# Whole 128x128 tiles in place of the half tiles of 64 in an attention and expert kernel

## The chip, the cores and the metric

The kernel runs on one core of one Trainium2 chip. The metric is the device time of one execution in microseconds (us). The core's engines each run an instruction queue of their own, in order: TensorE (in the profile PE, its weight loads PEld), VectorE (DVE), ScalarE (ACT), GpSimd (POOL) and SyncE (SP), which issues the transfers.

## The reference

Three stages follow one another on 8 batches of 576 tokens: attention over keys and values that are averaged in groups of 8, four causal attention experts of which each token takes two, and a mixing of tokens and channels.

```python
# attention: 8 heads, 576 queries, 72 pooled keys
k_p = k.reshape(B, H, Sp, pool, D).mean(axis=3)
scores = scale * np.matmul(q, k_p.transpose(0, 1, 3, 2))
attn = softmax(scores)
x = np.matmul(attn, v_p)
# experts: 4 of them, each with one causal head of 64
for e in range(E):
    a = softmax(causal(scale * (x @ wq[e]) @ (x @ wk[e]).T))
    out += gate[e] * (a @ (x @ wv[e]) @ wo[e])
# mixing
theta = x @ w_theta
y = w_tok_r @ (x * cos(theta)) + w_tok_i @ (x * sin(theta))
u = x + y
out = u + max(u @ w_ch, 0)
```

## The kernel before

A planner (class `Plan`) records every instruction with what it reads and writes, and a price for each (`price`). `issue` then takes the instructions in the order in which a model of the engines would run them: the earliest modelled start first, and of several the lowest key. Keys come from two tables, `PARTS` and `SHIFT`, that stand in the file as constants. What comes out is one fixed order for each engine. As all instructions are issued at one place in `issue`, the profile gives line L413 to all of them, and they are told apart by the names of their tiles.

Each batch goes through stage A (the first attention), the projections, and stage B (the experts). The planner weaves stage B of batch b with stage A and the projections of batch b + 1. Stage C (the mixing) comes last, for all batches; the weights of its stage are decoded earlier, in between.

576 is 4 times 128 and 64 more. So each batch ends in a half tile:

- `load_q` loads the queries in five tiles, `qraw`. The fifth has 64 queries.
- `attn_half` takes each tile of queries: 4 float32 products of the queries with the pooled keys (`s<-kbd,qraw`, the queries being the weights that TensorE holds, each product two matmul instructions), the exponentials in `pp`, then the normalised probabilities `pm` (64 keys of each of 8 heads) and `pq` (the other 8 keys). TensorE transposes them, four times 128 columns of `pm` and one time 64 columns of `pq`, into `t`; from there ScalarE and VectorE write the two exact parts of `pa` and of `pr`. `pq` is a tile of 64 columns for every tile of queries, so its transpose uses half of the array's columns in all five. The fifth tile works with 64 rows.
- `proj_v` makes the values `v` and the gates' logits by tile of tokens: 12 matmuls `acc<-wvs,xT` in each tile, with 64 columns in the fifth.
- `turn` transposes the experts' probabilities (`pev`, `pod`) into `pt0`, `pt1`; the last 64 keys of the last 64 queries (i = 8) become `pt2`, a tile of 64 partitions, by a transpose of 64 columns.
- `heads` multiplies them with the values: matmuls `acc<-pt,v`, and for the last 64 keys four matmuls of 64 rows and 64 moving columns in each of the two pairs of experts, by 2 parts and 2 experts.

In the profile's forms, 128\*128 are the rows and columns of the array that an instruction uses; 128\*64 uses half of the columns, 64\*128 half of the rows, and 64\*64 half of both. In stage C the last 64 tokens of two batches are put together, so that no half tile is left there.

Of the kernel before, what the change touches and what calls it, by code (L numbers as in the profile page):

```python
# [20 lines left out]
S = 576  # L21
# [74 lines left out]
class View:  # L96
    """a tile that is made when its first instruction is issued, or a part of it"""
# [50 lines left out]
class Pool:  # L148
    """a tile pool that is opened and closed among the instructions"""
# [44 lines left out]
class Plan:  # L194
    """Records the instructions with what they read and write, and issues them in the order in which a
    model of the engines would run them: the earliest start first, of several the lowest key."""
# [59 lines left out]
        # a bank is taken only when what empties it can go ahead  # L256
# [19 lines left out]
        # the time in which the weights of a product come in, while the one before it runs  # L276
# [55 lines left out]
    # from the end of an instruction to the start of one of another engine (in TensorE, of its weights' load)  # L332
# [10 lines left out]
    def issue(self):  # L343
# [4 lines left out]
        # the tiles of a ring are taken in turn, but for those of PSUM  # L348
# [17 lines left out]
        while len(order) < len(self.ops):  # L366
# [21 lines left out]
            if o.eng == "PE":  # L388
                # the clock is halved after a stretch of little work
# [29 lines left out]
def body(ctx: ExitStack, tc, qT, kT, vm, vr, wqk, wvg, wo, woT, wth, wtok, wch, out):  # L419
# [8 lines left out]
    def mm3(acc, lhs, rhs, first, last):  # L428
        """acc += lhsᵀ rhs, each operand as its two exact parts"""
# [50 lines left out]
    # ---------------------------------------------------------------- loads of one batch  # L480
    ld = {}

    def load(b):
        """the loads of one batch; those of the first take buffers that have no use yet, to wait for nothing"""
# [14 lines left out]
        def load_q():  # L499
            for o in range(0, S, 128):  # L500
                t = awork.tile([128, 4, 128], F32, name="qraw", bufs=3)
                m = min(128, S - o)
                D.dma_start(t[:, :, :m], qT[b][:, :, o:o + m])
# [27 lines left out]
    # ---------------------------------------------------------------- constants  # L531
    # what the scores of 64 queries get: NEG in the last 64 columns where the key comes after the query
# [5 lines left out]
    # hm[8 h' + k, h] = 1 where h' = h, for each half of the partitions  # L538
# [8 lines left out]
    # before[e, j] = 1 where j < e  # L547
# [16 lines left out]
    pt2 = [keep.tile([64, 2, 64], F32R, name=f"pt2{c}") for c in range(2)]  # L564
# [6 lines left out]
    # ---------------------------------------------------------------- weights of the first two stages  # L571
# [26 lines left out]
        # the sign, and 0 where float32 has no such number  # L598
# [15 lines left out]
    # the weights that are decoded early, in slack time, and kept in DRAM till they are wanted  # L614
# [11 lines left out]
    # ---------------------------------------------------------------- stage A  # L626
# [42 lines left out]
    def attn_half(b, h, rb):  # L669
        q0, n = HALF[h]  # L670
        tiles = [(o, min(128, n - o)) for o in range(0, n, 128)]
        pa = [awork.tile([128, 4, 320], F32R, name=f"pa{c}", bufs=1) for c in range(2)]
        pr = awork.tile([128, 320], F32R, name="pr", bufs=1)
        for o, m in tiles:
# [3 lines left out]
            for c in range(2):  # L678
                s_ = ps.tile([128, 512], F32, name="s", bufs=4)[:m, :288]
                for p in (2 * c, 2 * c + 1):  # L680
                    T.matmul(s_[:, (p % 2) * 144:(p % 2) * 144 + 144], ld[b][1][(q0 + o) // 128][:, p, :m],
# [3 lines left out]
                V.tensor_reduce(mx[:m], sv, axis=AX.X, op=OP.max, negate=True)  # L685
                if (q0 + o) // 128 in WHOLE[b > 0]:
                    V.tensor_tensor(pp[:m, 4 * c:4 * c + 4], sv, mx[:m, :, None].to_broadcast([m, 4, 72]), op=OP.add)
                    continue
                V.tensor_scalar(mx[:m], mx[:m], 1.0 / 64, None, op0=OP.mult)
                for g in range(4):  # L690
                    A.activation(pp[:m, 4 * c + g], sv[:, g], AF.Exp, bias=mx[:m, g:g + 1], scale=1.0 / 64,
                                 accum_out=l[:m, 4 * c + g:4 * c + g + 1])
            if (q0 + o) // 128 in WHOLE[b > 0]:
                A.activation(pp[:m], pp[:m], AF.Exp, scale=1.0 / 64)
                V.tensor_reduce(l[:m], pp[:m], axis=AX.X, op=OP.add)
            V.tensor_scalar(l[:m], l[:m], 1e-9, 8.0, op0=OP.add, op1=OP.mult)
            V.reciprocal(l[:m], l[:m])
            pm = awork.tile([128, 8, 64], F32, name="pm")
            pq = awork.tile([128, 8, 8], F32, name="pq")
            X = on(b, f"pm{(q0 + o) // 128}")  # L700
            X.tensor_tensor(pm[:m], pp[:m, :, 0:64], l[:m, :, None].to_broadcast([m, 8, 64]), op=OP.mult)
            X.tensor_tensor(pq[:m], pp[:m, :, 64:72], l[:m, :, None].to_broadcast([m, 8, 8]), op=OP.mult)
            pl.lane = "qt"
            t4 = ps.tile([128, 4, 128], F32, name="t")
            for p in range(4):
                T.transpose(t4[:, p, :m], pm[:m, 2 * p:2 * p + 2].rearrange("q g k -> q (g k)"), ident[:m, :m])
            A.copy(pa[0][:, :, o:o + m], t4[:, :, :m])
            V.tensor_tensor(pa[1][:, :, o:o + m], t4[:, :, :m], f(pa[0][:, :, o:o + m]), op=OP.subtract)
            t1 = ps.tile([128, 4, 128], F32, name="t")
            T.transpose(t1[:64, 0, :m], pq[:m].rearrange("q g k -> q (g k)"), ident[:m, :m])  # L710
            A.copy(pr[0:64, o:o + m], t1[:64, 0, :m])
            V.tensor_tensor(pr[64:128, o:o + m], t1[:64, 0, :m], f(pr[0:64, o:o + m]), op=OP.subtract)
# [11 lines left out]
    # ---------------------------------------------------------------- projections  # L724
# [28 lines left out]
    def proj_v(b, hs=(0, 1)):  # L753
# [4 lines left out]
        for t in [t for h in hs for t in ((0, 1), (2, 3, 4))[h]]:  # L758
            h, o = (0, 128 * t) if t < 2 else (1, 128 * t - 256)
            m = 128 if t < 4 else 64  # L760
            acc = ps.tile([128, 512], F32, name="acc")
            for kt in range(4):
                mm3(acc[:m, :260], [x[:, kt, o:o + m] for x in xT[b, h]], [w[:, kt] for w in wv_s],
                    kt == 0, kt == 3)
            a = [acc[:m, 128 * p:128 * p + 128].rearrange("k (e d) -> k e d", e=2) for p in range(2)]
            for p in range(2):
                A.copy(v[p][:m, t, :, 0], a[p])
            for p in range(2):
                V.tensor_tensor(v[p][:m, t, :, 1], a[p], f(v[p][:m, t, :, 0]), op=OP.subtract)
            V.tensor_copy(lg[:m, t], acc[:m, 256:260])  # L770
# [30 lines left out]
    # ---------------------------------------------------------------- stage B  # L801
    cnt = [0, 0]

    def scores(b, p, i, l):
# [8 lines left out]
        for c0, m in parts:  # L813
# [7 lines left out]
            # a = -(a + mask), and the lowest of it  # L821
# [6 lines left out]
    def norm(b, p, units, l):  # L828
        """divides the exponentials of one or two units by their sums, and weighs them with the gates"""
# [10 lines left out]
    def turn(b, p, i, pb, c0):  # L840
# [12 lines left out]
        if i == 8:  # L853
            t = ps.tile([128, 4, 128], F32, name="t")
            T.transpose(t[:64, 0], pb[:, 512:576], ident)
            src = t[:64, 0].rearrange("k (e q) -> k e q", e=2)
            A.copy(pt2[0], src)
            V.tensor_tensor(pt2[1], src, f(pt2[0]), op=OP.subtract)

    def heads(b, p, h):  # L860
# [5 lines left out]
        for e in range(2):  # L866
# [74 lines left out]
    # ---------------------------------------------------------------- stage C  # L941
# [17 lines left out]
    # wo w_theta, which takes the gated heads straight to theta  # L959
# [18 lines left out]
    def loadc(b):  # L978
# [7 lines left out]
        if b % 2 == 0:  # L986
            # the last 64 queries of two batches
# [11 lines left out]
    def mix(b):  # L999
        """x2, theta and the turned x2 of one batch"""  # L1000
# [156 lines left out]
```

## Time and profile before

| | |
|---|---|
| median of 3 runs | 1006.52 us (1005.34 to 1011.48) |
| span of the profiled execution | 1006.9 us |
| PE busy | 941.3 us (93%) |
| DVE busy | 692.6 us (69%) |
| ACT busy | 577.2 us (57%) |
| POOL busy | 519.4 us (52%) |

The span is that of one execution taken by the profiler. The ends of matmuls are modelled, each some 0.2 to 0.4 us after its start, so PE counts as busy while it only waits for a pipeline; what a matmul costs its queue is the time from its start to the start of the next one, which the timeline shows. The timeline merges instructions of one kind that follow each other: start, length from the first start to the last end, and the count.

### The profile page before, as it was taken

The page shows a single profiled execution, that of the slowest core. Times are in us where ns is not written, and L with a number is a line of the kernel's source. Part 1 is how long each engine was busy: PE and PEld are TensorE (multiplying, and loading weights), DVE is VectorE, ACT ScalarE, POOL GpSimd, SP SyncE. Part 2 cuts the span into 40 slices and gives each one's busy share as a digit, 9 for nine tenths or more (in the row PEclk, how much of TensorE's full clock was granted, in tenths as well). Part 3 has the DMA queues.
Part 4 walks back from the last instruction along what each step waited for, and adds up shares of the span by engine and source line. Part 5 has one row for each costly group of instructions (what it writes and reads, how often), then busy time and mean ns, then how long its engine had stood idle before and what let it go on. Part 6 is the DMA issues. An engine that isn't in the chain of part 4 may idle for free.

```text
span 1006.9 us, 19100 instructions
## 1 busy us (share of the span) xinstructions
PE 941.3 (93%) x6512; PEld 873.5 (87%) x6512; DVE 692.6 (69%) x1939; ACT 577.2 (57%) x1824; POOL 519.4 (52%) x641
## 2 busy tenths in 40 slices
PE   4889899999999999999998998999999999999998
PEld 3778789898888888989976798988999899999998
DVE  8899988989877898787779956174535726264421
ACT  4468777877868688686667634153434534353420
POOL 8877667574865837534254665352444435161420
PEclk9999999999999999999999999999999999999999
DMA  8444244343433422312175412020020202010001
GB/s 264 134 127 134 90 119 125 97 127 99 125 98 92 123 74 58 101 38 83 35 251 189 153 54 84 1 68 27 30 61 13 77 1 69 1 36 13 30 19 48
DMA packets 72033, 84.81 MB, mean 84 GB/s; under 512 B 14080, under 2 KB 54528, under 8 KB 71936
## 3 DMA queue, kind: packets, MB, share of 16 engines
q1 hardware_dynamic: 71936, 83.59, 28.2%
q8 instruction: 52, 0.85, 0.3%
q14 instruction: 45, 0.37, 0.1%
HBM read 57.29 MB, written 26.28 MB: 83 GB/s over the span
## 4 chain that ended last, share of the span: by engine, by line
PE 56%; DVE 28%; ACT 6%; issue 3%; POOL 3%; DMA 3%; SPq 0%; DVEq 0%; POOLq 0%; ACTq 0%
PE acc L413 42%; PE s L413 10%; PE t L413 4%; DVE s L413 3%; DVE zf L413 2%; DVE pt L413 2%; DVE d_raw L413 2%; DVE mx L413 2%; DVE th L413 2%; DVE r L413 2%; ACT th L413 1%; DVE qbd L413 1%; DMA d_raw<-in_wch_dram 1%; DMA vraw<-in_vm_dram 1%; DVE pa L413 1%
## 5 line engine op out<-in xcount | busy, mean ns | idle before, releaser
L413 PE MATMUL acc<-toks,z 128*128 128x288 f32 x1536 | 229.2, 296 | 2.0 <-DVE z L413 1.6
L413 PEld LDWEIGHTS acc<-toks,z 128*128 128x128 f32 x1536 | 215.3, 188 | 7.1 <-DVE z L413 2.0
L413 PE MATMUL acc<-xT,wqs 128*128 128x256 f32 (+1 forms) x768 | 136.4, 307 | 12.8 <-DVE qbd L413 8.9
L413 POOL TENSOR_TENSOR us<-u,us 128x288 fp32r<-128x288 f32 x64 | 54.9, 858 | 142.6 <-ACT us L413 142.6
L413 PEld LDWEIGHTS acc<-xT,wqs 128*128 128x128 f32 x768 | 109.0, 189 | 17.9 <-issue 10.8
L413 POOL TENSOR_TENSOR z<-zf,z 128x512 fp32r<-128x512 f32 x60 | 83.3, 1403 | 76.5 <-ACT z L413 76.5
L413 PE MATMUL acc<-us,chs 128*128 128x288 f32 x768 | 118.7, 301 | 3.7 <-ACT chs L413 1.9
L413 PEld LDWEIGHTS acc<-us,chs 128*128 128x128 f32 x768 | 110.6, 190 | 9.5 <-ACT chs L413 2.5
L413 DVE TENSOR_TENSOR u<-acc,xt 128x288 f32<-128x288 f32 x64 | 29.1, 455 | 119.8 <-PE acc L413 119.7
L413 PE MATMUL s<-kb,qbd 128*128 128x288 f32 (+8 forms) x480 | 110.7, 326 | 0.6 <-ACT kb L413 0.6
L413 POOL TENSOR_SCALAR pev<-pev,lb,G 128x64 f32<-128x64 f32 (+4 forms) x80 | 50.7, 634 | 99.6 <-DVE lb L413 40.4
L413 ACT CAST us<-u 128x288 fp32r<-128x288 f32 x64 | 27.6, 431 | 111.4 <-DVE u L413 111.1
L413 PE MATMUL acc<-pt,v 128*128 128x320 f32 (+3 forms) x448 | 80.6, 299 | 3.7 <-ACT pt L413 1.1
L413 ACT ACTIVATE pp<-s,mx 128x72 f32<-128x72 f32 (+1 forms) x232 | 73.3, 328 | 14.8 <-DVE mx L413 13.3
L413 PEld LDWEIGHTS acc<-pt,v 128*128 128x128 f32 (+1 forms) x448 | 68.5, 189 | 14.4 <-ACT pt L413 2.1
L413 ACT CAST pt<-t 128x512 fp32r<-128x512 f32 (+4 forms) x160 | 66.7, 431 | 23.3 <-PE t L413 21.9
L413 DVE TENSOR_TENSOR pt<-t,pt 128x512 fp32r<-128x512 f32 (+4 forms) x160 | 75.1, 482 | 6.1 <-ACT pt L413 5.5
L413 DVE CUSTOM_DVE_ANT_0 s<-s,mask 128x64 f32<-128x64 f32 (+2 forms) x144 | 65.6, 459 | 17.6 <-PE s L413 16.9
L413 PEld LDWEIGHTS s<-kb,qbd 128*128 128x128 f32 x480 | 74.6, 190 | 2.7 <-ACT kb L413 0.8
L413 PE MATMUL acc<-wvs,xT 128*128 128x260 f32 (+1 forms) x480 | 71.2, 290 | 2.6 <-DVE logit L413 1.9
L413 PE MATMUL s<-kbd,qraw 128*128 128x144 f32 (+1 forms) x320 | 62.4, 306 | 8.2 <-POOL hm L413 6.8
L413 PEld LDWEIGHTS acc<-wvs,xT 128*128 128x128 f32 (+1 forms) x480 | 60.7, 179 | 4.3 <-issue 1.8
(171 smaller groups left out, 2211.3 us busy)
## 6 DMA issues: line engine op xcount, KB each, us to landing
out_dram<-o SPq DMA_DIRECT2D x64, 144.0 KB, 1.8
kraw<-in_kT_dram SPq DMA_DIRECT2D x15, 576.0 KB, 4.2
qraw<-in_qT_dram SPq DMA_DIRECT2D x32, 256.0 KB, 3.3
yraw<-ygD SPq DMA_DIRECT2D x16, 512.0 KB, 4.0
vraw<-in_vm_dram SPq DMA_DIRECT2D x15, 512.0 KB, 4.4
d_raw<-in_wtok_dram SPq DMA_DIRECT2D x18, 288.0 KB, 2.9
toks<-tokD SPq DMA_DIRECT2D x18, 288.0 KB, 5.5
ygD<-yg SPq DMA_DIRECT2D x32, 160.0 KB, 2.6
```

The source lines that it names most:

```text
L413: o.ins = o.fn(*[a.real() if isinstance(a, View) else a for a in o.args], **{k: a.real() if isinstance(a, View) else a for k, a in o.kw.it ...
```

## The change

Every half tile becomes a whole one. The fifth tile of queries, keys and tokens starts 64 earlier, at 448, and covers tokens 448 to 575, of which the first 64 are done a second time and not used again (`n_` picks the new ones; the logits take partitions 64 to 127). `pt2` gets 128 partitions, of which the first 64 are zero, set once at the start. `pq` gets 128 columns, of which the last 64 are zero, set once; it is no longer taken from a ring of two but is one of two fixed tiles, by the parity of the tile of queries. The transposes are then 128 by 128. `PARTS`, `SHIFT` and the planner stay as they were. What of the diff takes comments out is not shown.

```diff
         def load_q():
...
-                m = min(128, S - o)
-                D.dma_start(t[:, :, :m], qT[b][:, :, o:o + m])
+                o = min(o, S - 128)
+                D.dma_start(t, qT[b][:, :, o:o + 128])
...
-    pt2 = [keep.tile([64, 2, 64], F32R, name=f"pt2{c}") for c in range(2)]
+    pt2 = [keep.tile([128, 2, 64], F32R, name=f"pt2{c}") for c in range(2)]
+    for t in pt2:
+        P.memset(f(t[:64]), 0.0)
+    pqs = [keep.tile([128, 2, 8, 8], F32, name=f"pq{c}") for c in range(2)]
+    for t in pqs:
+        P.memset(t[:, 1], 0.0)
...
     def attn_half(b, h, rb):
...
-        for o, m in tiles:
+        for o, new in tiles:
...
-                    T.matmul(s_[:, (p % 2) * 144:(p % 2) * 144 + 144], ld[b][1][(q0 + o) // 128][:, p, :m],
+                    T.matmul(s_[:, (p % 2) * 144:(p % 2) * 144 + 144], ld[b][1][(q0 + o) // 128][:, p],
                              kbd[:, p].rearrange("d e k -> d (e k)"), start=True, stop=True)
...
-            pq = awork.tile([128, 8, 8], F32, name="pq")
+            pq = pqs[(q0 + o) // 128 % 2]
...
-            X.tensor_tensor(pq[:m], pp[:m, :, 64:72], l[:m, :, None].to_broadcast([m, 8, 8]), op=OP.mult)
+            X.tensor_tensor(pq[:, 0], pp[:, :, 64:72], l[:, :, None].to_broadcast([128, 8, 8]), op=OP.mult)
             pl.lane = "qt"
+            n_ = slice(128 - new, 128)
             t4 = ps.tile([128, 4, 128], F32, name="t")
             for p in range(4):
-                T.transpose(t4[:, p, :m], pm[:m, 2 * p:2 * p + 2].rearrange("q g k -> q (g k)"), ident[:m, :m])
+                T.transpose(t4[:, p], pm[:, 2 * p:2 * p + 2].rearrange("q g k -> q (g k)"), ident)
...
-            T.transpose(t1[:64, 0, :m], pq[:m].rearrange("q g k -> q (g k)"), ident[:m, :m])
-            A.copy(pr[0:64, o:o + m], t1[:64, 0, :m])
+            T.transpose(t1[:, 0], pq.rearrange("q w g k -> q (w g k)"), ident)
+            A.copy(pr[0:64, o:o + new], t1[:64, 0, n_])
...
     def proj_v(b, hs=(0, 1)):
...
-            h, o = (0, 128 * t) if t < 2 else (1, 128 * t - 256)
-            m = 128 if t < 4 else 64
+            h, o = (0, 128 * t) if t < 2 else (1, min(128 * t, S - 128) - 256)
...
-                mm3(acc[:m, :260], [x[:, kt, o:o + m] for x in xT[b, h]], [w[:, kt] for w in wv_s],
+                mm3(acc[:, :260], [x[:, kt, o:o + 128] for x in xT[b, h]], [w[:, kt] for w in wv_s],
...
     def turn(b, p, i, pb, c0):
...
-            T.transpose(t[:64, 0], pb[:, 512:576], ident)
+            T.transpose(t[:, 0], pb[:, 448:576], ident)
...
     def heads(b, p, h):
...
-                    T.matmul(acc[:, 256:320], v[:64, 4, e], pt2[c][:, e], start=False, stop=c == 1)
+                    T.matmul(acc[:, 256:320], v[:, 4, e], pt2[c][:, e], start=False, stop=c == 1)
```

## Rows read from the trace of the kernel before

**Rows 1.** The page: busy time, share of the span and instructions.

```profile
PE 941.3 (93%) x6512; PEld 873.5 (87%) x6512; DVE 692.6 (69%) x1939; ACT 577.2 (57%) x1824; POOL 519.4 (52%) x641
```

**Rows 2.** The page: the chain that ended last, by engine.

```profile
PE 56%; DVE 28%; ACT 6%; issue 3%; POOL 3%; DMA 3%; SPq 0%; DVEq 0%; POOLq 0%; ACTq 0%
```

**Rows 3.** Windows, one batch: length, then PE, PEld, DVE, ACT, POOL busy, clock, DMA.

```profile
299.00:361.00 62.00, 57.13 (x419) 52.91 (x418) 51.83 (x187) 45.84 (x185) 37.79 (x54) 1.00 0.36 103
```

**Rows 4.** Groups by shape: busy, mean ns | idle before; whole and half tiles.

```profile
L413 ACT ACTIVATE pp<-s,mx 128x72 f32<-128x72 f32 x176 | 56.0, 333 | 13.4 <-DVE mx L413 11.9 <-DVE logit L413 1.2
...
L413 PEld LDWEIGHTS acc<-wvs,xT 128*128 128x128 f32 x384 | 48.4, 190 | 1.6 <-DVE xT L413 1.0 <-PE acc L413 0.2
...
L413 ACT ACTIVATE pp<-s,mx 64x72 f32<-64x72 f32 x56 | 17.3, 314 | 1.4 <-DVE mx L413 1.4
...
L413 PE MATMUL acc<-pt,v 64*128 64x64 f32 x64 | 15.0, 287 | 0.0
...
L413 PE MATMUL s<-kbd,qraw 128*64 128x144 f32 x64 | 13.2, 306 | 0.0
...
L413 PEld LDWEIGHTS acc<-wvs,xT 128*64 128x64 f32 x96 | 12.4, 135 | 2.8 <-issue 1.8 <-PE acc L413 0.6
```

**Rows 5.** Timeline of PE, where half tiles of two kinds alternate.

```profile
314.16 0.46 PE L413 MATMUL s<-kbd,qraw 128*64 128x144 f32 x2
314.55 0.36 PE L413 MATMUL acc<-pt,v 128*128 128x192 f32 x1
314.84 0.46 PE L413 MATMUL s<-kbd,qraw 128*64 128x144 f32 x2
...
318.84 0.30 PE L413 MATMUL t<-ident,pq 128*64 128x128 f32 x1
319.07 0.29 PE L413 MATMUL acc<-pt,v 64*128 64x64 f32 x1
319.29 1.55 PE L413 MATMUL acc<-xT,wqs 128*128 128x256 f32 x11
```

**Rows 6.** Timeline of PE: whole tiles of 144 and of 64 moving columns.

```profile
272.35 0.78 PE L413 MATMUL s<-kb,qbd 128*128 128x64 f32 x6
272.96 0.71 PE L413 MATMUL s<-kbd,qraw 128*128 128x144 f32 x4
...
305.62 0.90 PE L413 MATMUL s<-kbd,qraw 128*128 128x144 f32 x6
306.26 0.37 PE L413 MATMUL acc<-pa,vbd 128*128 128x256 f32 x1
```

**Rows 7.** Timeline of PE: eight half matmuls of the queries in a row.

```profile
190.67 1.20 PE L413 MATMUL s<-kbd,qraw 128*64 128x144 f32 x8
191.79 0.63 PE L413 MATMUL acc<-xT,wqs 128*128 128x256 f32 x3
```

**Rows 8.** The chain in order of time, over the stretch of rows 5.

```profile
313.12 1.11 PE acc L413 x8
314.23 0.39 PE s L413 x2
...
319.14 0.24 PE acc L413
```

**Rows 9.** Timeline of DVE: what it waits for behind that stretch.

```profile
320.01 0.28 DVE L413 TENSOR_TENSOR pr<-t,pr 64x128 fp32r<-64x128 f32 x1 [1.86 <-ACT pr L413]
```

**Rows 10.** Transfers of queries, whole and half: KB each, us to landing.

```profile
qraw<-in_qT_dram SPq DMA_DIRECT2D x32, 256.0 KB, 3.3
...
qraw<-in_qT_dram SPq DMA_DIRECT2D x8, 128.0 KB, 2.6
```

**Rows 11.** Timeline of POOL at the start: a small memset, and the first wait.

```profile
7.17 0.10 POOL L413 MEMSET logit<- 64x4 f32 x1
...
13.19 0.72 POOL L413 TENSOR_TENSOR vt<-pm 128x256 f32<-128x256 f32 x1 [2.87 <-DVE vbd L413]
```

**Rows 12.** Waits of PE, 80 to 500 us: total, times, longest (us).

```profile
PE acc L413 <- DVE qbd L413: 6.0, 6, 1.6
```

More of the change, by code (lines that the diff above doesn't have):

```diff
@@ L678, in attn_half @@
             for c in range(2):
-                s_ = ps.tile([128, 512], F32, name="s", bufs=4)[:m, :288]
+                s_ = ps.tile([128, 512], F32, name="s", bufs=4)[:, :288]
                 for p in (2 * c, 2 * c + 1):
-                    T.matmul(s_[:, (p % 2) * 144:(p % 2) * 144 + 144], ld[b][1][(q0 + o) // 128][:, p, :m],
+                    T.matmul(s_[:, (p % 2) * 144:(p % 2) * 144 + 144], ld[b][1][(q0 + o) // 128][:, p],
                              kbd[:, p].rearrange("d e k -> d (e k)"), start=True, stop=True)
@@ L684, in attn_half @@
                 mx = awork.tile([128, 4], F32, name="mx", bufs=4)
-                V.tensor_reduce(mx[:m], sv, axis=AX.X, op=OP.max, negate=True)
+                V.tensor_reduce(mx, sv, axis=AX.X, op=OP.max, negate=True)
                 if (q0 + o) // 128 in WHOLE[b > 0]:
-                    V.tensor_tensor(pp[:m, 4 * c:4 * c + 4], sv, mx[:m, :, None].to_broadcast([m, 4, 72]), op=OP.add)
+                    V.tensor_tensor(pp[:, 4 * c:4 * c + 4], sv, mx[:, :, None].to_broadcast([128, 4, 72]), op=OP.add)
@@ L688, in attn_half @@
                     continue
-                V.tensor_scalar(mx[:m], mx[:m], 1.0 / 64, None, op0=OP.mult)
+                V.tensor_scalar(mx, mx, 1.0 / 64, None, op0=OP.mult)
                 for g in range(4):
-                    A.activation(pp[:m, 4 * c + g], sv[:, g], AF.Exp, bias=mx[:m, g:g + 1], scale=1.0 / 64,
-                                 accum_out=l[:m, 4 * c + g:4 * c + g + 1])
+                    A.activation(pp[:, 4 * c + g], sv[:, g], AF.Exp, bias=mx[:, g:g + 1], scale=1.0 / 64,
+                                 accum_out=l[:, 4 * c + g:4 * c + g + 1])
@@ L693, in attn_half @@
             if (q0 + o) // 128 in WHOLE[b > 0]:
[L694 to L697, printed above, removed]
+                A.activation(pp, pp, AF.Exp, scale=1.0 / 64)
+                V.tensor_reduce(l, pp, axis=AX.X, op=OP.add)
+            V.tensor_scalar(l, l, 1e-9, 8.0, op0=OP.add, op1=OP.mult)
@@ L698, in attn_half @@
+            V.reciprocal(l, l)
             pm = awork.tile([128, 8, 64], F32, name="pm")
-            pq = awork.tile([128, 8, 8], F32, name="pq")
+            pq = pqs[(q0 + o) // 128 % 2]
             X = on(b, f"pm{(q0 + o) // 128}")
-            X.tensor_tensor(pm[:m], pp[:m, :, 0:64], l[:m, :, None].to_broadcast([m, 8, 64]), op=OP.mult)
-            X.tensor_tensor(pq[:m], pp[:m, :, 64:72], l[:m, :, None].to_broadcast([m, 8, 8]), op=OP.mult)
+            X.tensor_tensor(pm, pp[:, :, 0:64], l[:, :, None].to_broadcast([128, 8, 64]), op=OP.mult)
@@ L703, in attn_half @@
+            X.tensor_tensor(pq[:, 0], pp[:, :, 64:72], l[:, :, None].to_broadcast([128, 8, 8]), op=OP.mult)
             pl.lane = "qt"
+            n_ = slice(128 - new, 128)
             t4 = ps.tile([128, 4, 128], F32, name="t")
             for p in range(4):
-                T.transpose(t4[:, p, :m], pm[:m, 2 * p:2 * p + 2].rearrange("q g k -> q (g k)"), ident[:m, :m])
-            A.copy(pa[0][:, :, o:o + m], t4[:, :, :m])
-            V.tensor_tensor(pa[1][:, :, o:o + m], t4[:, :, :m], f(pa[0][:, :, o:o + m]), op=OP.subtract)
+                T.transpose(t4[:, p], pm[:, 2 * p:2 * p + 2].rearrange("q g k -> q (g k)"), ident)
@@ L709, in attn_half @@
+            A.copy(pa[0][:, :, o:o + new], t4[:, :, n_])
+            V.tensor_tensor(pa[1][:, :, o:o + new], t4[:, :, n_], f(pa[0][:, :, o:o + new]), op=OP.subtract)
             t1 = ps.tile([128, 4, 128], F32, name="t")
-            T.transpose(t1[:64, 0, :m], pq[:m].rearrange("q g k -> q (g k)"), ident[:m, :m])
-            A.copy(pr[0:64, o:o + m], t1[:64, 0, :m])
-            V.tensor_tensor(pr[64:128, o:o + m], t1[:64, 0, :m], f(pr[0:64, o:o + m]), op=OP.subtract)
+            T.transpose(t1[:, 0], pq.rearrange("q w g k -> q (w g k)"), ident)
@@ L713, in attn_half @@
+            A.copy(pr[0:64, o:o + new], t1[:64, 0, n_])
+            V.tensor_tensor(pr[64:128, o:o + new], t1[:64, 0, n_], f(pr[0:64, o:o + new]), op=OP.subtract)
         pl.lane = "pv"
@@ L758, in proj_v @@
         for t in [t for h in hs for t in ((0, 1), (2, 3, 4))[h]]:
-            h, o = (0, 128 * t) if t < 2 else (1, 128 * t - 256)
-            m = 128 if t < 4 else 64
+            h, o = (0, 128 * t) if t < 2 else (1, min(128 * t, S - 128) - 256)
             acc = ps.tile([128, 512], F32, name="acc")
             for kt in range(4):
-                mm3(acc[:m, :260], [x[:, kt, o:o + m] for x in xT[b, h]], [w[:, kt] for w in wv_s],
+                mm3(acc[:, :260], [x[:, kt, o:o + 128] for x in xT[b, h]], [w[:, kt] for w in wv_s],
                     kt == 0, kt == 3)
-            a = [acc[:m, 128 * p:128 * p + 128].rearrange("k (e d) -> k e d", e=2) for p in range(2)]
+            a = [acc[:, 128 * p:128 * p + 128].rearrange("k (e d) -> k e d", e=2) for p in range(2)]
             for p in range(2):
-                A.copy(v[p][:m, t, :, 0], a[p])
+                A.copy(v[p][:, t, :, 0], a[p])
             for p in range(2):
-                V.tensor_tensor(v[p][:m, t, :, 1], a[p], f(v[p][:m, t, :, 0]), op=OP.subtract)
-            V.tensor_copy(lg[:m, t], acc[:m, 256:260])
+                V.tensor_tensor(v[p][:, t, :, 1], a[p], f(v[p][:, t, :, 0]), op=OP.subtract)
+            if t < 4:
+                V.tensor_copy(lg[:, t], acc[:, 256:260])
+            else:
+                V.tensor_copy(lg[:64, t], acc[64:128, 256:260])
         if 1 not in hs:
@@ L854, in turn @@
             t = ps.tile([128, 4, 128], F32, name="t")
-            T.transpose(t[:64, 0], pb[:, 512:576], ident)
-            src = t[:64, 0].rearrange("k (e q) -> k e q", e=2)
-            A.copy(pt2[0], src)
-            V.tensor_tensor(pt2[1], src, f(pt2[0]), op=OP.subtract)
+            T.transpose(t[:, 0], pb[:, 448:576], ident)
+            src = t[64:128, 0].rearrange("k (e q) -> k e q", e=2)
+            A.copy(pt2[0][64:128], src)
+            V.tensor_tensor(pt2[1][64:128], src, f(pt2[0][64:128]), op=OP.subtract)
     def heads(b, p, h):
```

## The prediction

> **What bounds the kernel now.** I read the page first, then the windows, the groups by shape, and the timeline of PE where half tiles stand. The page has PE busy for 93% of the span [rows 1], and the chain that ended last lies on PE for 56% and on DVE for 28% [rows 2]. PE is the bound, but not alone: in one batch of the woven part, 62 us long, PE is busy for 57.13 us and DVE for 51.83 us [rows 3], and the chain goes to and fro between them. Busy time of PE does not say what a matmul costs, as ends are modelled. So I go by the distance from one start to the next.
>
> There the half tiles stand out. Where halves of columns (`s<-kbd,qraw`) and halves of rows (`acc<-pt,v`) alternate, a pair of query matmuls holds the queue for 0.39 us (314.16 to 314.55) and one `acc<-pt,v` of 64 moving columns for 0.22 us (319.07 to 319.29) [rows 5]. The whole forms are quicker: six query matmuls take 0.64 us, or 0.21 us a pair, and six matmuls of 64 moving columns take 0.61 us, or 0.10 us each [rows 6]. None of these halves waits for an operand: idle time before both groups is 0.0 [rows 4]. The lost time goes with the change of shape itself. The reader should compare the eight halves in a row, 1.12 us or 0.14 us each [rows 7]: with no change of shape between them they cost little more than whole ones.
>
> **The change part by part.** All matmuls become 128\*128, so no change of shape is left. I price one batch.
>
> *Where kinds alternate (the stretch of rows 5).* Between 314.16 and 319.29 stand four pairs of query matmuls, one `acc<-pt,v` of 192 columns between two of them, four `acc<-pt,v` of 64 and one transpose of `pq` (rows 5 show two of the pairs, the one of 192, one of the four and the transpose).
> - query pairs: 4 x (0.39 - 0.21) = 0.72 us [rows 5, 6].
> - `acc<-pt,v` of 64: 4 x (0.22 - 0.10) = 0.48 us [rows 5, 6].
> - the one of 192 columns: 0.29 us now (314.55 to 314.84). Whole and among whole ones it costs at least the 0.107 us of 144 columns [rows 6] and at most that by its columns, 0.107 x 192 / 144 = 0.14 us; I take 0.12, so 0.17 us.
> - the transpose of `pq`: 0.23 us now (318.84 to 319.07); whole, its 128 columns lie between the 0.10 and the 0.107 us of rows 6; I take 0.10, so 0.13 us.
>
> That is 1.50 us. *Where they don't alternate*: the eight in a row save 8 x (0.14 - 0.107) = 0.26 us [rows 6, 7], and I add one entry of 0.17 us, as for the 192 columns: about 0.45 us.
>
> How often is it the one or the other? The union of all 64 query halves is 13.2 us [rows 4]. 32 pairs that stand alone would make 32 x 0.46 = 14.7 us [rows 5], 8 groups of eight 8 x 1.20 = 9.6 us [rows 7]. So (13.2 - 9.6) / (14.7 - 9.6) = 0.7 of them alternate. A batch then saves 0.7 x 1.50 + 0.3 x 0.45 = 1.19 us, and eight of them 9.5 us.
>
> *Is that on the path?* In the stretch it is: the chain of waits stays on PE from 313.12 to 319.38 without a break [rows 8]. What is late next is the work behind it, on ACT and DVE: DVE waits 1.86 us for the `pr` that comes out of this very stretch [rows 9], and has 62 - 51.8 = 10 us idle in a batch [rows 3]. A gain of 1.2 us a batch fits in, so I count it whole.
>
> *The second group of four `acc<-pt,v` in each batch* (64 in all, eight a batch [rows 4]) is not in that stretch. If they stand in pairs they pay two entries of 0.17 us, 0.3 us a batch, 2.4 us in all; I take it at PE's share of the chain, 0.56 [rows 2]: 1.3 us. Bounds: 0 and 2.4 us.
>
> *The other transposes of half tiles* (the fifth tile's five, and `pev`'s two, a batch). I read none of them on the chain and take 0. Bounds: a whole one costs 0.10 us [rows 6] where a half one could cost nothing, on five of them 0.5 us a batch or 4 us in all; and a gain of 0.13 us, as for the `pq` of rows 5, on six of them a batch, 6.2 us in all, if a lone change of shape costs as much as one between two kinds of halves.
>
> *`proj_v`.* 96 matmuls with 64 columns [rows 4]; the moving columns, 260, stay. The weight load goes from 135 to 190 ns [rows 4]. It runs beside the matmul before it, and in whole tiles the same 190 ns stand beside the same 260 columns in 384 instructions with 1.6 us idle in all [rows 4]. I take 0. Bounds: a gain of one entry of 0.17 us a batch, 1.4 us; a loss of 96 x 0.055 = 5.3 us if the cover were gone.
>
> *Exponentials, sums, copies.* They keep their elements in each partition and take 128 partitions in place of 64, or 64 at another place. The exponentials show the price: 314 ns on 64 partitions, 333 on 128 [rows 4], so 56 x 0.019 = 1.1 us. ACT, busy for 45.84 of 62 us [rows 3], hides it; I take 0, with bounds 0 and 1.1 us.
>
> *Loads.* The fifth load of a batch has 256 KB in place of 128 and lands after 3.3 in place of 2.6 us [rows 10]. It is issued a batch ahead, on SP's queue, so those 0.7 us are hidden; with no cover they would be lost in the first batch alone. I take 0; bounds 0 and 0.7 us.
>
> *Four memsets on POOL at the start,* 0.10 us or a little more each [rows 11], ahead of `kt` and `kbd`. POOL waits 2.87 us shortly after [rows 11]. I take 0; bounds 0 and 0.5 us. The fixed `pq` tiles come free a tile of queries later at most; a batch lies between the two uses of one buffer that follow each other at a batch's end, so 0.
>
> Sum: 9.5 + 1.3 = 10.8 us. 1006.9 - 10.8 = 996.1 us; the profiled execution lies 0.4 us above the median of the runs (1006.52), so I say 996.0.
>
> **The rivals.**
> 1. *The gain is taken back by DVE.* It is busy 51.83 of 62 us [rows 3] and 28% of the chain is on it [rows 2]. If its order, not PE's, sets the pace in most batches, what PE saves turns into PE waits. For it: the chain leaves PE right behind the stretch. Against: the 1.86 us of rows 9. The chain's share of DVE is half that of PE [rows 2], and I take it that DVE then lets through only the third that falls where DVE waits: 3.6 us; 1003 us.
> 2. *The order gets worse (slower).* The planner sorts by modelled starts with keys that were set for the old sizes. It prices a load of weights by its columns and a transfer by its bytes, so `pq`, `pev`, `proj_v` and the fifth `qraw` move in its model, and the order may shift from there on. PE's queue is in order: one matmul that is put ahead of its operand blocks all behind it, as `acc` does now behind `qbd`, 1.6 us at the longest [rows 12]. Seven such waits (10.8 / 1.6) eat the gain; at 14 of them, nearly two a batch, it is 1006.9 - 10.8 + 22.4 = 1018.5 us. Against: prices of matmuls don't change, and now there are six such waits in 420 us, 6.0 us together.
> 3. *The change does not do what it says*: the 0.39 us is not for the shape but for something that stays, for instance the float32 products themselves next to the others. Against: whole float32 pairs next to other kinds in rows 6 don't show it (0.21 us). Time: 1006.5 us.
> 4. *Half tiles are the cheaper form.* If half tiles side by side shared the array, or if weight loads set the pace, whole tiles would lose: (96 + 64) x 0.055 = 8.8 us [rows 4], 1015.7 us. Against: eight halves in a row take 0.14 us each, whole ones 0.107 [rows 6, 7]. The Trainium skill (TensorEngine Tiling (Array Packing), Theoretical Speedup) has this rule: a dimension of 64 or less allows up to twice the speed. No run here shows halves that overlap.
> 5. *Every change of shape costs, the lone transposes' too.* Then the 6.2 us above come on top: 1006.9 - 10.8 - 6.2 = 989.9 us. For it: the `pq` of rows 5 pays. Against: it stands between halves of rows, and I read no price of a lone one. The Trainium skill (TensorEngine Tiling (Array Packing), Key Properties) has this as a rule: a change of the tiling mode, not of the tile alone, drains TensorE. By that rule it is this rival's time, by rows 5 to 7 alone the forecast's; rows 5 agree with it, 0.39 against 0.21 us.
>
> **How the numbers follow.** The forecast has 0.54, DVE 0.19, the order 0.09, no effect 0.07, halves cheaper 0.03, every change 0.08. The forecast alone reaches from 990 us (all stretches alternate: 12 us; the second group whole: 2.4 us; 1.4 us from `proj_v`: 15.8, with a little rounding) to 1004 us (no stretch alternates as read, 8 x 0.45 = 3.6 us, and 0.7 us at the start); rival 5 on top of the larger bounds reaches some 985. About 1% is what a measurement of this kernel can tell from no change, that is 996.4 us. Some 0.65 of the forecast's chance lies on the faster side, since its bounds at 0 hold more gains than losses that nothing hides; with rival 5 that makes 0.43. The rest of it, DVE and no effect make 0.45 within 1%; the order and the cheaper halves 0.12 slower. The range goes from 987 to 1008 us: it leaves out the two slower cases, 0.12, and some 0.05 below.
>
> **What would show it.** In the changed kernel no form with 64 in rows or columns of the array is left. The query matmuls of the fifth tile should stand 0.21 us a pair and `acc<-pt,v` of 64 columns 0.10 us apart; a batch of the woven part should be some 60.6 us in place of 62; busy time of DVE should stay as it is. If PE's waits for DVE grow by about the time saved, it was rival 1; if single waits of over 1 us appear in PE's list, rival 2; if pairs still take 0.39 us, rival 3. The prediction is wrong if a batch keeps its length though the pairs got shorter.

## The result, and the profile after

The changed kernel is slower: 1018.66 us (median of 4 runs, 1015.04 to 1021.17) against 1006.67 us before, a ratio of 1.0115 with a 95% interval of 1.0081 to 1.015. The forecast was 996 us, 1% the other way. The profiled execution of the changed kernel has a span of 1013.3 us.

The page of the changed kernel, busy time and the chain by engine (as [rows 1] and [rows 2]):

```profile
PE 934.1 (92%) x6512; PEld 875.8 (86%) x6512; DVE 709.2 (70%) x1939; ACT 579.4 (57%) x1824; POOL 516.0 (51%) x645
...
PE 46%; DVE 29%; ACT 13%; issue 4%; DMA 3%; POOL 3%; DVEq 0%; POOLq 0%; ACTq 0%; SPq 0%
```

PE is busy for 7 us less [rows 1]. DVE has the same 1939 instructions and is busy for 17 us more. The share of the chain on PE fell from 56% to 46%, and ACT's rose from 6% to 13% [rows 2]. That shift is no sign of the loss: in the experiments below, whole tiles in the order of before are faster with PE at 47% and ACT at 12%, and half tiles in the new order are slower with PE at 57% and ACT at 6%.

What the change set out to do, it did. Groups by shape of the changed kernel (busy, mean ns, idle before):

```profile
L413 PE MATMUL s<-kbd,qraw 128*128 128x144 f32 x320 | 62.4, 303 | 10.0 <-DVE kbd L413 7.1 <-POOL kbd L413 2.6 <-ACT pev L413 0.3
...
L413 PE MATMUL acc<-pt,v 128*128 128x64 f32 x64 | 10.7, 247 | 0.0
```

All 320 query matmuls have one form, and the 64 matmuls of 64 moving columns take 10.7 us of busy time in place of 15.0 [rows 4]. No form with 64 rows or columns of the array is left.

The loss is elsewhere, and begins early. The window from 60 to 80 us, before and then after (columns as in [rows 3]):

```profile
60.00:80.00 20.00, 17.08 (x116) 15.39 (x117) 18.34 (x64) 15.04 (x64) 12.70 (x20) 1.00 0.30 89
```

```profile
60.00:80.00 20.00, 15.76 (x90) 14.42 (x90) 16.82 (x54) 11.00 (x42) 9.81 (x17) 0.83 0.26 79
```

It held 116 matmuls at full clock, and now holds 90 at a granted clock of 0.83, where 1.0 is full speed (90 at 0.91 in another execution of the changed kernel, of the experiments below). PE's timeline there:

```profile
59.67 2.80 PE L413 MATMUL acc<-xT,wqs 128*128 128x320 f32 x18
62.31 0.65 PE L413 MATMUL s<-kbd,qraw 128*128 128x144 f32 x4
66.65 6.09 PE L413 MATMUL acc<-xT,wqs 128*128 128x320 f32 x24 [3.69 <-DVE qbd L413]
72.58 0.27 PE L413 MATMUL t<-ident,pev 128*128 128x128 f32 x1
```

PE stood still for 3.69 us until VectorE had written `qbd`, and the 24 matmuls behind it took 6.09 us. VectorE's timeline just before shows what stood ahead of `qbd`:

```profile
61.61 1.98 DVE L413 TENSOR_TENSOR cmp<-cmp,gt 128x80 f32<-128x80 f32 x1
63.52 1.22 DVE L413 TENSOR_SCALAR d_s<-d_raw 128x256 f32<-128x256 f32 x1
64.66 0.22 DVE L413 TENSOR_REDUCE sel<-cmp 128x20 f32<-128x80 f32 x1
64.81 0.67 DVE L413 TENSOR_SCALAR d_raw<-d_raw 128x256 int32<-128x256 int32 x1
65.51 0.99 DVE L413 SCALAR_TENSOR_TENSOR qbd<-acc,qbd 64x320 fp32r<-64x320 f32 x2
```

Two steps of decoding a later stage's weights (`d_s`, `d_raw`) stand ahead of `qbd`. Neither `qbd` nor the 24 matmuls are instructions that the change touches. That is a matter of the order, and the order is not part of the diff: it is what the planner makes of changed prices.

### The profile page after: what moved, and what is told of

Same layout as the page of the kernel before. It is cut to its first block, busy times and chain, and to the rows that moved or that the text cites. A ratio compares the mean times of both kernels' runs of the same rounds, so it can differ in the third digit from the quotient of the medians.

```text
span 1013.3 us, 19058 instructions
## 1 busy us (share of the span) xinstructions
PE 934.1 (92%) x6512; PEld 875.8 (86%) x6512; DVE 709.2 (70%) x1939; ACT 579.4 (57%) x1824; POOL 516.0 (51%) x645
## 4 chain that ended last, share of the span: by engine, by line
PE 46%; DVE 29%; ACT 13%; issue 4%; DMA 3%; POOL 3%; DVEq 0%; POOLq 0%; ACTq 0%; SPq 0%
PE acc L413 35%; PE s L413 8%; ACT pp L413 4%; PE t L413 3%; DVE s L413 3%; DVE d_raw L413 2%; DVE pt L413 2%; DVE zf L413 2%; DVE mx L413 2%; ACT pev L413 2%; DVE th L413 2%; DVE r L413 2%; DVE qbd L413 1%; ACT pt L413 1%; ACT th L413 1%
## 5 line engine op out<-in xcount | busy, mean ns | idle before, releaser
L413 PE MATMUL acc<-xT,wqs 128*128 128x256 f32 (+1 forms) x768 | 138.8, 315 | 9.8 <-DVE qbd L413 9.6
L413 PEld LDWEIGHTS acc<-xT,wqs 128*128 128x128 f32 x768 | 113.5, 196 | 12.5 <-issue 9.9
L413 ACT ACTIVATE pp<-s,mx 128x72 f32<-128x72 f32 x232 | 73.9, 334 | 16.7 <-DVE mx L413 16.1
L413 PE MATMUL acc<-wvs,xT 128*128 128x260 f32 x480 | 71.2, 292 | 4.6 <-DVE logit L413 3.4
L413 PE MATMUL acc<-pt,v 128*128 128x320 f32 (+3 forms) x448 | 69.9, 292 | 3.8 <-ACT yg L413 2.3
L413 PEld LDWEIGHTS acc<-pt,v 128*128 128x128 f32 x448 | 64.1, 191 | 9.2 <-ACT yg L413 5.0
L413 PE MATMUL s<-kbd,qraw 128*128 128x144 f32 x320 | 62.4, 303 | 10.0 <-DVE kbd L413 7.1
L413 PEld LDWEIGHTS acc<-wvs,xT 128*128 128x128 f32 x480 | 63.4, 190 | 7.3 <-PE acc L413 1.8
```

Source lines behind the costliest of these rows:

```text
L413: o.ins = o.fn(*[a.real() if isinstance(a, View) else a for a in o.args], **{k: a.real() if isinstance(a, View) else a for k, a in o.kw.it ...
```

## The experiments

The theories. A: whole tiles save about what the trace of before shows, and the planner, which gets other prices for them, puts out an order that costs more. B: the whole tiles themselves cost. Both kernels could be had in both orders, since with the same keys the planner's order follows from its prices. The ratios and intervals are those on record; they are not quotients of the two medians, and differ from them by up to 0.08%.

**Whole tiles in the order of before.** The planner is told the old prices of what used to be half: weight loads at half, the fifth load of queries at 450 ns. The order is that of before on TensorE, VectorE, ScalarE and in the transfers; on GpSimd the four memsets come in at the start, and two instructions for the mask change places with others there.

```diff
         if eng == "PE":
             w = args[1]
             o.load = int(np.prod(w.box.shape[1:])) * (0.1 if w.root.dtype == BF else 0.84)
+            if self.half:
+                o.load /= 2
         o.cost = self.price(eng, method, outs, ins, args, kw)
+        if o.kind == "DMA.qraw" and self.half:
+            o.cost = 450.0
```

(`self.half` is set around the five places that the change makes whole.)

> The changed kernel, with whole tiles everywhere, but the planner is told the prices of the half tiles (loads of weights of 64 columns, and 450 ns for the fifth load of queries), so that it puts out the order of the kernel before, instruction for instruction, on TensorE, VectorE, ScalarE and the transfers; on GpSimd only the four memsets come in between at the start. Theory A (whole tiles save what the trace of before shows, and the new order costs more than that): 993 to 1000 us, ratio 0.987 to 0.993. Theory B (the whole tiles themselves cost more than the halves, the order is of no weight): 1014 to 1021 us, as the changed kernel.

Measured: 998.53 us against 1007.98 us of before, ratio 0.9906 (0.9884 to 0.9928). B falls: the whole tiles save 9.5 us. On another chip, beside the last experiment below:

> Whole tiles in the order of before, once more, on the same chip as the newly set keys: 996 to 1001 us by every theory.

997.59 us against 1005.55, ratio 0.9923 (0.99 to 0.9946), 8.0 us.

**Half tiles in the order of the changed kernel.** The kernel before; only the planner's prices are the new ones.

```diff
-            o.load = int(np.prod(w.box.shape[1:])) * (0.1 if w.root.dtype == BF else 0.84)
+            o.load = max(128, int(np.prod(w.box.shape[1:]))) * (0.1 if w.root.dtype == BF else 0.84)
         o.cost = self.price(eng, method, outs, ins, args, kw)
+        if o.kind == "DMA.qraw":
+            o.cost = 256 * 1024 / 350.0
```

> The kernel before, with its half tiles, but the planner is told the prices of whole tiles, so that it puts out the order of the changed kernel on TensorE, VectorE, ScalarE and the transfers. Theory A: the order alone costs some 20 us, and the half tiles keep their stalls: 1020 to 1032 us. Theory B: 1005 to 1009 us, as before.

Measured: 1023.57 us, ratio 1.016 (1.0141 to 1.0179). Not one instruction of it differs from before but in its place, and it is 1.6% slower. The order alone costs 15.6 us. Beside the two, the changed kernel again:

> The changed kernel once more, on the same chip as the three others: 1014 to 1021 us by every theory.

1018.05 us, ratio 1.0093 (1.0067 to 1.0118). The four make a square, as ratios to before: half tiles 1 and 1.016 in the two orders, whole tiles 0.9906 and 1.0093. The tiles give 0.9% or 0.7%, the order takes 1.6% or 1.9%.

**Is it this order, or any other one?** A price that has nothing to do with the change:

```diff
             if method == "transpose":
-                return 113
+                return 116
```

> The kernel before with one price in the planner changed that has nothing to do with half tiles: a transpose at 116 in place of 113 ns. The instructions are the same, the order is another from the first batch on. Theory A in its general form (the keys fit one order, and any small step away from the prices that they were set with costs about as much): 1012 to 1028 us. Theory C (the order of the changed kernel is bad for something of its own, a price of whole tiles that is wrong): 1003 to 1010 us.

Measured: 1021.5 us, ratio 1.0135 (1.0117 to 1.0153). C falls: three nanoseconds on a transpose's price cost nearly as much as all the prices of the change (1.016). Then each half of the new prices alone, with whole tiles. The price of the fifth load (of the first edit above, the two lines on `o.cost` are left out, so that the price of `qraw` is the new one):

> The changed kernel with whole tiles, where the planner gets one new price alone: the fifth load of queries at the price of its 256 KB in place of 450 ns. The loads of weights keep the old prices. Its order leaves that of before at the 57th matmul. Theory A in its general form (any order but the one that the keys were set for costs some 15 us): 1008 to 1020 us. Theory C (the new prices of weight loads make the bad order): 997 to 1001 us.

Measured: 1009.15 us, ratio 1.0032 (1.0017 to 1.0047); some 1.1 to 1.3% above whole tiles in the order of before (0.9923 and 0.9906). And the weight loads' price alone (the two lines on `o.load` left out):

> The changed kernel with whole tiles, where the planner gets the new prices of weight loads alone; the fifth load of queries keeps its 450 ns. Its order leaves that of before at the 94th matmul. Theory A in its general form: some 8 to 20 us above the kernel in the order of before, 1006 to 1018 us. Theory D (the price of the transfer is what makes the bad order): 997 to 1001 us.

Measured: 1016.29 us, ratio 1.0088 (1.0071 to 1.0106), some 1.7 to 1.8% above. D falls too: either price is enough to lose what whole tiles bring. Four orders other than that of before, all with the keys as they were, and four losses of 1.1 to 1.9% against the same tiles in the order of before.

**Is the loss at places, or is it the bad start that throws the rest out of step?** Two kernels with whole tiles sort twice, with the old and with the new prices, and splice the orders after 1680 of 10587 instructions, at about 120 us:

```diff
+CUT = 1680
...
+        first, second = self.sort(0), self.sort(1)
+        first = first[:CUT]
+        done = set(first)
+        order = first + [o for o in second if o not in done]
```

> Whole tiles; the first 1680 of 10587 instructions (to about 120 us) in the order of before, the rest in the order of the changed kernel. Theory E (the loss stands at places: some 6 us in the first 120 us, the rest in the batches between 190 and 310 us): 1010 to 1014 us. Theory F (the bad start throws the rest out of step): 998 to 1003 us.

Measured: 1015.78 us, ratio 1.0083 (1.0057 to 1.0109). The other way round:

> Whole tiles; the first 1680 instructions in the order of the changed kernel, the rest in the order of before. Theory E: the 6 us of the first 120 us stay and nothing comes on top, 1002 to 1006 us. Theory F: 1012 to 1019 us.

Measured: 1006.12 us, ratio 1.0 (0.9986 to 1.0014). F falls, as both times lie some 6 us or more outside its ranges. E is nearer, but neither time lies in its ranges: the new order's first 120 us cost 0.9% (1.0 against 0.9906) with the old rest behind them, its rest 1.8% with the old start ahead. The first kernel came out 1.8 us above E's range, the second 0.1 us, and the two losses together are more than the 1.9% of the whole order; where two orders meet something may be lost too, which was not measured by itself.

**Are the keys to blame, or has the order of before something of its own?** The changed kernel as it is, with the new prices; only the constants of `PARTS` and `SHIFT` are set anew, fitted to the new prices by the planner's own modelled end.

```diff
-    "first": (-897.04, 230.28), "kv first": (-844.24, 2.16), ...
+    (other constants for the same names)
```

> The changed kernel as it is, with whole tiles and their new prices in the planner; only the constants in PARTS and SHIFT are set anew, fitted to these prices by the planner's own modelled end. The order is neither that of before nor that of the changed kernel. Theory A (keys fit one set of prices, and the loss of the changed kernel is theirs): most of the 19.5 us comes back, 996 to 1006 us. Theory G (the order of before is good by some property on the chip that the planner's model does not know): 1008 to 1020 us, as any other order.

Measured: 999.12 us against 1005.55, ratio 0.9933 (0.9913 to 0.9954). G falls: an order that was never that of before is as good within the intervals (0.9923 on the same chip), once the keys fit the prices. One such set of keys was tried. Three versions beat both kernels: whole tiles in the order of before, this one, and below the queries' tiles alone made whole.

**Which part brings the gain?** Each in the order of before. The queries' half tiles alone (load, scores, transposes of `pm` and `pq`):

> The order of before, and only the queries' half tiles made whole: the fifth load, its scores, the transposes of pm and pq. The half matmuls of rows with pt2 and of columns in proj_v stay. With whole queries the changes from half columns to half rows go, but a change to half rows and back stays. Theory A1 (the price is in the change between two kinds of halves): the larger part of the 9.5 us, 5 to 8 us, 1000 to 1003 us. Theory A2 (each kind pays for itself): some 4 to 5 us, 1003 to 1004 us.

Measured: 1002.54 us against 1006.71, ratio 0.9966 (0.9951 to 0.998). The values' alone (`proj_v`):

> The order of before, and only the values' half tiles of proj_v made whole (96 matmuls with 128 in place of 64 columns of weights). Both theories: no gain that can be measured, 1006 to 1008 us; if weight loads set the pace a loss of some 5 us.

Measured: 1009.18 us, ratio 1.0028 (1.0016 to 1.0041), a small loss where both theories had none, and less than the 5 us of the third case. And the values' with the last 64 keys' (`pt2`):

> The order of before, the values' and the last 64 keys' half tiles made whole (proj_v, pt2, its transposes, acc<-pt,v), the queries' left as halves. Theory A1: 5 to 8 us, 1000 to 1003 us, since here too no change between two kinds of halves is left. Theory A2: some 4 to 5 us, 1003 to 1004 us, and with the queries' part it adds up to the 9.5 us of both.

Measured: 1005.16 us, ratio 0.9989 (0.9973 to 1.0006), no change clear of the noise. Neither A1 nor A2 came out. The 1002.54 us of the queries lies in A1's range of times, but the gain of some 4 us is below its 5 to 8, and the keys are slower than either theory said. The queries bring 0.34%, the keys 0.39% over the values alone, `proj_v` by itself loses 0.28%, and the sum of it is 0.45%, against the 0.94% and 0.77% that all three bring together. What the parts show of the mechanism is in their traces, where only one kind of half is left. PE's timeline with whole queries and half keys, then with half queries and whole keys:

```profile
312.50 0.43 PE L418 MATMUL s<-kbd,qraw 128*128 128x144 f32 x2
312.86 0.29 PE L418 MATMUL acc<-pt,v 64*128 64x64 f32 x1
313.08 0.51 PE L418 MATMUL s<-kbd,qraw 128*128 128x144 f32 x2
313.52 0.29 PE L418 MATMUL acc<-pt,v 64*128 64x64 f32 x1
313.75 0.51 PE L418 MATMUL s<-kbd,qraw 128*128 128x144 f32 x2
```

```profile
315.79 0.30 PE L418 MATMUL acc<-pt,v 128*128 128x64 f32 x1
316.02 0.46 PE L418 MATMUL s<-kbd,qraw 128*64 128x144 f32 x2
316.41 0.30 PE L418 MATMUL acc<-pt,v 128*128 128x64 f32 x1
316.63 0.46 PE L418 MATMUL s<-kbd,qraw 128*64 128x144 f32 x2
```

Next to whole ones, a half-row matmul still holds the queue for 0.22 us (312.86 to 313.08), and a whole query pair in front of it for 0.44 (313.08 to 313.52). A half-column pair still takes 0.39 us (316.02 to 316.41), and the whole matmul in front of it 0.23. The half forms take the same 0.22 and 0.39 us as in the kernel before [rows 5]. So for these matmuls a change between half and whole costs as much as one between two kinds of halves; only when all are whole it goes. Over the stretch of rows 5, 5.13 us long before, whole queries alone save 0.40 us (312.14 to 316.87) and whole keys alone 0.56 us (314.73 to 319.30), 0.96 us together, where all of it whole saves 1.56 us (next section). That is one reason why the parts bring less than the whole. That it is the only one is not shown.

## Why the prediction was wrong

**The price of the stretch was right.** PE's timeline of the same stretch with whole tiles in the order of before:

```profile
312.77 0.43 PE L418 MATMUL s<-kbd,qraw 128*128 128x144 f32 x2
312.94 0.34 PE L418 MATMUL acc<-pt,v 128*128 128x192 f32 x1
313.13 0.43 PE L418 MATMUL s<-kbd,qraw 128*128 128x144 f32 x2
313.30 0.29 PE L418 MATMUL acc<-pt,v 128*128 128x64 f32 x1
313.43 0.49 PE L418 MATMUL s<-kbd,qraw 128*128 128x144 f32 x2
313.66 0.29 PE L418 MATMUL acc<-pt,v 128*128 128x64 f32 x1
...
316.15 0.33 PE L418 MATMUL t<-ident,pq 128*128 128x128 f32 x1
316.23 0.28 PE L418 MATMUL acc<-pt,v 128*128 128x64 f32 x1
316.34 1.54 PE L418 MATMUL acc<-xT,wqs 128*128 128x256 f32 x11
```

From the first query pair to the end it is 316.34 - 312.77 = 3.57 us, against 319.29 - 314.16 = 5.13 us before [rows 5]: 1.56 us saved where the prediction had 1.50.

**The sum of the tiles' part was right in size.** 10.8 us were forecast, 9.5 and 8.0 us measured in the order of before. (1006.9 less 10.8 and 0.4 is 995.7 us, not the 996.0 that the prediction wrote; nothing hangs on it.)

**That all of it passes through was right only as a mean.** Starts of the first `G` of each batch, from VectorE's timeline (us):

| batch | 0 | 1 | 2 | 3 | 4 | 5 | 6 | 7 |
|---|---|---|---|---|---|---|---|---|
| before | 66.9 | 119.0 | 179.1 | 240.2 | 302.1 | 364.9 | 428.0 | 484.3 |
| whole tiles, order of before | 67.1 | 119.7 | 179.2 | 240.5 | 300.8 | 361.0 | 421.9 | 476.2 |
| changed kernel | 68.7 | 125.6 | 186.5 | 251.5 | 316.2 | 377.1 | 439.3 | 491.9 |

Up to batch 3 whole tiles bring nothing, then 1.6, 2.6, 2.2 and 2.0 us a batch, where 1.2 to 1.4 were forecast for each. That the sum came out near 10 us is so in part luck. Rows 5 are of the later batches; what holds the earlier ones was not tried. The chain of waits from 240 to 300 us, before and with whole tiles in the same order, shows what comes next:

```profile
by line: PE acc L413 35.8%; PE s L413 12.0%; PE t L413 6.1%; DVE pt L413 5.9%; DVE s L413 5.5%; DVE d_raw L413 4.3%; DVE mx L413 4.2%; issue 2.7%; DVE xT L413 2.6%; DVE qbd L413 2.0%; DVE lb L413 1.9%; DVE l L413 1.7%; DVE g L413 1.7%; DVE 
```

```profile
by line: DVE s L418 10.4%; ACT pp L418 9.6%; PE acc L418 9.4%; DVE pt L418 7.7%; issue 5.6%; DVE d_raw L418 5.0%; DVE qbd L418 4.3%; DVE mx L418 4.3%; DVE lb L418 3.0%; DVE xT L418 3.0%; DVE pa L418 2.8%; ACT pt L418 2.5%; ACT pev L418 2.5%
```

PE's `acc` falls from 35.8% of that stretch to 9.4%, and VectorE and ScalarE take over. Rival 1 had named VectorE as the next, but with 3.6 us let through where it was 8.0 to 9.5, and without ScalarE beside it.

**The step that failed is the order.** The sum had a term for every instruction and none for the place of the instructions, though the prediction itself said that weight loads and the fifth transfer move in the planner's model. It stood as rival 2 with a chance of 0.09, on the ground that the prices of matmuls don't change. The runs show that each of the four changes of prices that were tried is enough: 1.1 to 1.9% in four orders, more than the tiles bring in any. Where the sum had nothing, the new order costs 15.6 us with half tiles (1023.57 against 1007.98) and 19.5 us with whole ones (1018.05 against 998.53). Rival 2 gave 1018.5 us and the result is 1018.66. It had the right cause, but that its number fits is luck, since the waits are not the ones it counted: 14 of 1.6 us, nearly two a batch. PE's waits from 80 to 500 us (as [rows 12]), the changed kernel and then whole tiles in the order of before:

```profile
PE acc L413 <- DVE qbd L413: 6.0, 7, 1.4
PE t L413 <- DVE pt L413: 4.0, 9, 1.1
PE acc L413 <- DVE logit L413: 3.7, 6, 0.8
PE t L413 <- DVE pa L413: 3.4, 3, 2.0
PE acc L413 <- ACT yg L413: 3.3, 5, 1.7
PE t L413 <- DVE pr L413: 3.2, 3, 1.5
```

```profile
PE acc L418 <- DVE qbd L418: 6.6, 5, 1.6
PE t L418 <- DVE mx L418: 2.8, 3, 0.9
PE acc L418 <- DVE logit L418: 2.6, 4, 1.6
PE acc L418 <- DVE xT L418: 2.4, 5, 1.2
PE t L418 <- DVE pt L418: 1.8, 4, 0.6
...
PE t L418 <- DVE pa L418: 1.1, 1, 1.1
```

The waits for `qbd` stay at 6 to 7 us; what grew are those for `pt`, `pa`, `pr` and `yg`, from 3.7 to 13.9 us together, 20 waits of 0.7 us on the mean. Others shrank (`mx` from 2.8 to 0.9 us), and all of PE's waits in that window add up to 31.5 us in 47 waits, against 24.6 us in 37. That growth of 6.9 us is less than the 10 us or so by which the changed kernel falls further behind from batch 1 to batch 7 in the table; where the rest goes was not tried. The one long wait, 3.69 us, stands before that window. The same place with whole tiles in the order of before, on PE and on VectorE:

```profile
64.70 5.29 PE L418 MATMUL acc<-xT,wqs 128*128 128x320 f32 x24 [2.08 <-DVE qbd L418]
```

```profile
60.95 2.00 DVE L418 TENSOR_TENSOR cmp<-cmp,gt 128x80 f32<-128x80 f32 x1
62.98 0.23 DVE L418 TENSOR_REDUCE sel<-cmp 128x20 f32<-128x80 f32 x1
63.25 0.17 DVE L418 TENSOR_SCALAR sel<-sel 128x20 f32<-128x20 f32 x1
63.46 0.48 DVE L418 SCALAR_TENSOR_TENSOR qbd<-acc,qbd 64x320 fp32r<-64x320 f32 x1
```

Here `qbd` comes ahead of the decoding; PE waits 2.08 in place of 3.69 us and the 24 matmuls take 5.29 in place of 6.09. (The `cmp` ahead is equally long in both, 2.00 and 1.98 us; what stretches such instructions is said at the end.) That is 2.4 of the 5.9 us by which the changed kernel is behind at batch 1 in the table. The 1.6 us of the wait are the order's; the 0.8 us of the matmuls are not sure to be, for in another execution of the changed kernel they took 5.29 us too, behind the same wait:

```profile
65.94 5.29 PE L413 MATMUL acc<-xT,wqs 128*128 128x320 f32 x24 [3.69 <-DVE qbd L413]
```

From batch 1 on the changed kernel loses 1.4, 3.7 and 4.4 us more up to batch 4, which was not taken apart wait by wait.

**The smaller terms.** `proj_v`, taken as 0 with a loss of up to 5.3 us, loses 0.28%, some 2.5 to 2.8 us, by itself; whether it does so among whole tiles too was not tried. The memsets and the fixed `pq` tiles were not tried by themselves; whatever they cost is inside the 997.6 to 998.5 us of whole tiles in the order of before. DVE's busy time, which was to stay as it is, rose from 692.6 to 696.8 us with whole tiles in the order of before, and to 708.6 us with half tiles in the new order: most of the rise goes with the order. Rival 3 and rival 4 fall with whole tiles in the order of before. Rival 5 had half of the mechanism right: single half matmuls between whole ones pay (the two timelines of the parts). But its 6.2 us more took 0.13 us for each of six lone transposes a batch, and those of half the columns do not pay it. PE's timeline with half queries and whole keys, where a half `pq` stands between two whole matmuls:

```profile
319.02 0.28 PE L418 MATMUL acc<-pt,v 128*128 128x64 f32 x1
319.13 0.30 PE L418 MATMUL t<-ident,pq 128*64 128x128 f32 x1
319.19 0.28 PE L418 MATMUL acc<-pt,v 128*128 128x64 f32 x1
```

It holds the queue for 0.06 us, where it was 0.23 us between halves of rows [rows 5] and is 0.08 us as a whole one (316.15 to 316.23 above). The fifth tile's transposes, of 64 rows, were not priced by themselves.

## What to carry to other kernels

Where a planner sorts by modelled times, a change of sizes is two changes, one of the instructions and one of the order; give the order a term of its own in the sum, and a width of its own in the range, before the instructions are priced. To try such a change, first hold the order (tell the planner the old prices), and only then let it sort anew, with keys set for the new prices. And read the cost of a half tile from the distances between starts next to it, in both directions, for busy times hide it.

## What the runs showed of the hardware

A change between half and whole tiles cost TensorE 0.1 to 0.2 us even in the whole matmul next to it. A whole query pair between two half-row matmuls took 0.44 us (313.08 to 313.52), and 0.23 us (313.43 to 313.66) where its neighbours were whole; a whole `acc<-pt,v` of 64 columns in front of a half-column pair took 0.23 us (315.79 to 316.02), and 0.13 us (313.30 to 313.43) in front of a whole one. The Trainium skill's rule that a change of the tiling mode drains TensorE (TensorEngine Tiling (Array Packing), Key Properties) agrees with both. The lone half-column transpose, at 0.06 us, shows no such cost; why it differs was not tried.

At one place a wait of PE cost more than its length. In the changed kernel 18 matmuls `acc<-xT,wqs` of 320 columns ahead of the wait of 3.69 us took 0.147 us each (59.67 to 62.31). Behind it 24 of the same form took 0.247 us each (66.65 to 72.58), with a granted clock of 0.57 over that stretch, which lies between the lower (1.2 GHz, 0.5) and the upper (2.4 GHz, 1.0) of the two levels. So 2.4 us were added to a wait of 3.69. That the wait brought the clock down is read from what came first, and was not tested by itself. In the other execution of the same kernel it was 1.6 us behind the same wait, at 0.67 (65.94 to 71.07). In the kernel before PE waited at this place too, for 1.67 us, and the 24 matmuls took 3.76 us at full clock:

```profile
64.53 3.76 PE L413 MATMUL acc<-xT,wqs 128*128 128x320 f32 x24 [1.67 <-DVE qbd L413]
```

VectorE's instructions are not equally long at every place. The first step of decoding, in groups by shape, before and after:

```profile
L413 DVE TENSOR_SCALAR d_s<-d_raw 128x256 f32<-128x256 f32 x16 | 7.2, 448 | 7.4 <-DMA d_raw<-in_wch_dram 7.4
```

```profile
L413 DVE TENSOR_SCALAR d_s<-d_raw 128x256 f32<-128x256 f32 x16 | 8.9, 558 | 9.1 <-DMA d_raw<-in_wch_dram 7.7 <-DMA d_raw<-in_wth_dram 1.3
```

The same 16 instructions take 558 ns in place of 448 on the mean, the one in front of `qbd` 1220 ns. Not all of that is the order's: in the order of before the same mean lies between 349 ns (the queries' tiles alone whole) and 505 ns (whole tiles), and in the new order between 498 ns (half tiles) and 563 ns (the changed kernel again). The traces show what the long ones stood beside. In the kernel before, 11 of the 16 began while no GpSimd `TENSOR_TENSOR` was under way, and took 0.24 to 0.32 us. Of the five that began inside one, four ended 0.15 to 0.16 us after it did: the longest, of 1.85 us, ended at 551.51 us, and GpSimd's `ys` had run from 548.68 to 551.36 us. Beside the one of 1.22 us, from 63.52 to 64.74 us, three of GpSimd's `vt` followed one another from 63.46 to 64.91 us. So the order also seems to decide which VectorE steps GpSimd holds up; no run changed this alone.
